# Query transposes of one batch moved from DMA to TensorE, and DMA engines put into the planned order, in a block-sorted attention with a bilinear feed-forward layer

## The chip, the cores and the metric

The kernel runs on one core of a Trainium2 chip. A core has five engines that each work through their own list of instructions in order: TensorE (PE, matmuls into PSUM banks), VectorE (DVE), ScalarE (ACT), GpSimd (POOL) and SyncE (SP). Here SP computes nothing and only issues DMAs; GpSimd issues DMAs too, besides tensor work. The DMAs of both are carried out by the core's 16 DMA engines. The metric is the device time of one execution in microseconds (us), lower is better.

## The reference

The inputs are q, k and v of shape (4 batches, 8 heads, 768 positions, 64), a matrix `sort_net` of 8 x 8 for each batch and head, and three weights of a feed-forward layer. Cut to what matters:

```python
P = sort_net
for _ in range(5):                      # rows, then columns, made to sum to one
    P = exp(P - P.max(-1)); P = P / P.sum(-1); P = P / P.sum(-2)
k_sorted = einsum('bhij,bhjcd->bhicd', P, k_b)      # blocks of 96 positions, mixed by P
v_sorted = einsum('bhij,bhjcd->bhicd', P, v_b)
attn = softmax(q_b @ k_sorted^T / 8)                # each block attends to its own block
x = (attn @ v_sorted) -> (4*768 tokens, 8*64)
out = ((x @ w_a) * (x @ w_b)) @ w_out               # 512 -> 1536 -> 512
```

## The kernel before

**Tiles and stages.** The work goes batch by batch (b = 0 to 3). In each, attention is done for four pairs of heads (p = 0 to 3), two heads of 64 filling the 128 partitions. For one pair, k and v are mixed by P on TensorE (`mix_pe` L480, `v_tok` L530), the query is transposed so that the head dimension lies on the partitions, scores and exponentials are made in two halves of four blocks (`scores_pe` L564, `exp_act` L578), the product with v follows (`o_pe` L585), and DVE normalizes it into a buffer `xp` (L594, L598). A transpose puts `xp` into `xT`, the input of the feed-forward layer.

**The feed-forward layer.** Batch 0 is done plainly (`ab_plain` L741). Batches 1 to 3 use a scheme of seven block products instead of eight (`ab_strassen` L806), with sums of the weights made once on GpSimd (`w_sums` L765) and sums of `xT` made for each batch (`x_sums` L785). The last product (`out_plain` L889) makes six output tiles per batch, and each is stored with two DMAs on SP (L915). While the outputs of batch b are made, attention of batch b+2 is done between them, and then the Strassen products of batch b+1 follow.

**How v and q travel.** For batches 1 to 3, v is mixed with positions on the partitions, copied out of PSUM by DVE, written to DRAM by a DMA on SP (`v_out` L540) and read back in another layout by a second one (`v_back` L544). The write-and-read is one round trip, both legs in SP's queue. `xp` of these batches is transposed by a DMA on SP (`x_dma` L615). The query has two ways. In batches 0 and 1 it is loaded plainly (L402), transposed on TensorE against an identity matrix (`q_pe` L463) and copied out of PSUM (`q_copy` L474). In batches 2 and 3 (`QDMA`, L194) it is loaded with the two heads interleaved (`q_wide` L350, two DMAs of small pieces for a pair of heads) and transposed by a DMA on SP (`q_dma` L620); `scores_pe` then reads it with another stride.

**What sets the order.** No engine's order is written by hand. Each piece of work is an `Op` with an engine or a choice of engines, an estimated duration, a latency until its result can be used, dependencies, buffers that it takes (`get`) and gives back (`put`), and a rank. `Plan.solve` (L132) simulates: it repeatedly takes the piece that can start first, and among those that can start within a small margin of one another (`EPS`, L40) the one of lowest rank. The resulting times are thrown away; the order stays, and `emit` (L988) writes every engine's instructions in that order. On the chip each engine follows its list and waits where a wait is due, however the real durations turn out. So a change of an estimate changes the order of real instructions on all engines.

GpSimd's loads are two pieces in the plan: an issue on POOL and a transfer on a made-up engine "DQ", `nbytes / 333e3` us long (`load`, L311), one transfer at a time. DMAs on SP, before the change, are one piece on SP with a fixed latency behind it; they do not occupy DQ. SP's stretch for a q transpose is 1.8 us with 3.6 us of latency (L662), for an x transpose 1.35 and 2.6 (L724), for the v write 0.5 and the default 2.3, for the v read 0.7 and 3.5 (L642, L643).

Of the kernel before, what the change touches and what calls it, by code (L numbers as in the profile page):

```python
# [35 lines left out]
class Plan:  # L36


    LAT = {"NIL": 0.0, "PE": 0.21, "ACT": 0.07, "DVE": 0.07, "POOL": 0.1, "SP": 2.3, "DQ": 1.9}
    EPS = {"NIL": 0.0, "PE": 0.08, "ACT": 0.04, "DVE": 0.04, "POOL": 0.04, "SP": 0.04, "DQ": 0.0}  # L40

    AT = {"NIL": 0.0, "PE": 0.8, "ACT": 2.05, "DVE": 0.8, "POOL": 1.25, "SP": 0.7, "DQ": 1.5}

# [5 lines left out]
    def add(self, eng, dur, fn, deps=(), get=(), put=(), rank=0.0, lat=None):  # L49
        alts = dict(eng) if isinstance(eng, (list, tuple)) else {eng: dur}  # L50
        op = Op(alts, fn, deps, list(get), list(put), rank, lat, len(self.ops))
        for key in op.put:
            self.holders[key] = self.holders.get(key, 0) + 1
        self.ops.append(op)
        return op
# [135 lines left out]

STRASSEN_AB = (1, 2, 3)
STRASSEN_OUT = ()
QDMA = lambda b, p: b >= 2  # L194
VDMA = lambda b, p: b >= 1


# [1 line left out]
def kernel(  # L199
# [40 lines left out]
    add = plan.add  # L240
# [70 lines left out]
    def load(fn, nbytes, deps=(), get=(), rank=0.0, many=0.0):  # L311
        ds = [d for d in deps if d is not None] + ([ld_n[-7]] if len(ld_n) >= 7 else [])
        i = add("POOL", 0.72 + many, fn, ds, get=get, rank=rank, lat=0.0)
        d = add("DQ", nbytes / 333e3, None, [i], rank=rank)
        ld_n.append(d)
        return d

    o_p = add("SP", 0.1, lambda: nc.sync.dma_start(
        out=p_nat, in_=sort_net.rearrange("b h i j -> (b h) i j")), lat=1.5)
    o_im = add("DVE", 0.1, lambda: nc.vector.memset(ident, 0.0))  # L320
# [17 lines left out]
    o_pads = add("DVE", 1.0, pads, rank=1)  # L338


    q_in, k_in, v_in = {}, {}, {}
# [8 lines left out]
    def q_wide(b, p):  # L350
        t = buf(("q2", b, p))
        for e in range(2):
            nc.gpsimd.dma_start(
                out=_ap(t, e * D, [[2 * W, P], [2 * D, NCH], [1, D]]),
                in_=_ap(q, (b * H + 2 * p + e) * S * D, [[W, P], [D, NCH], [1, D]]))
# [6 lines left out]
    NB_KV = 2 * S * D * 4  # L362
# [31 lines left out]
    def load_pair(b, p, rank, after=None):  # L394
        for name, t, into in (("k2", k, k_in), ("v2", v, v_in)):
            into[b, p] = load(lambda name=name, t=t: kv(b, p, name, t), NB_KV, [after],
                              get=[(name, (name, b, p))], rank=rank)
        if QDMA(b, p):
            q_in[b, p] = load(lambda: q_wide(b, p), NB_KV * 1.5, [after],
                              get=[("q2", ("q2", b, p))], rank=rank, many=0.9)  # L400
        else:
            q_in[b, p] = load(lambda: nc.gpsimd.dma_start(  # L402
                out=buf(("q2", b, p)),
                in_=_ap(q, (b * H + 2 * p) * S * D, [[W, P], [S * D, 2], [1, W]])), NB_KV,
                get=[("q2", ("q2", b, p))], rank=rank)
# [39 lines left out]
    for p in range(1, HP):  # L445
# [3 lines left out]
        put=["pc"], rank=-7)  # L449
# [175 lines left out]
    def mix_part(b, p, rk, split):  # L625

        pair = ("pair",)
        tc_o = VDMA(b, p)
        km = add("PE", 0.46, lambda: mix_pe(b, p, "k"), [k_in[b, p], s_ok[b, p]],
                 get=[("pair", ("km", b, p))], put=[("k2", b, p)], rank=rk)  # L630
        ks = []
        for h in ((0, 1) if split else (None,)):
            ks.append(add("ACT", 0.48 if split else 0.8,
                          lambda h=h: mix_copy("ACT", b, p, "k", h, tc_o), [km, o_pads] + ks,
                          get=[("kT", ("kT", b, p))] if not ks else [], put=[("km", b, p)],
                          rank=rk + (0.3 if h == 1 else 0)))
        if tc_o:
            vm = add("PE", 0.33, lambda: v_tok(b, p), [v_in[b, p], s_ok[b, p]],
                     get=[("pair", ("vm", b, p))], put=[("v2", b, p)], rank=rk)
            vc = add("DVE", 0.95, lambda: v_tok_copy("DVE", b, p), [vm],  # L640
                     get=[("vm", ("vb", b, p))], put=[("vm", b, p)], rank=rk)
            vo = add("SP", 0.5, lambda: v_out(b, p), [vc], put=[("vb", b, p)], rank=rk)  # L642
            vb = add("SP", 0.7, lambda: v_back(b, p), [vo, o_pads], get=[("vs", ("vs", b, p))],  # L643
                     rank=rk, lat=3.5)
            return ks, [vb]
        vm = add("PE", 0.46, lambda: mix_pe(b, p, "v"), [v_in[b, p], s_ok[b, p]],
                 get=[("pair", ("vm", b, p))], put=[("v2", b, p)], rank=rk + 0.05)
        vs = []
        for h in ((0, 1) if split else (None,)):
            alts = (("DVE", 0.56), ("ACT", 0.48)) if split else (("DVE", 0.95), ("ACT", 0.8))  # L650
            op = add(alts, None, None, [vm, o_pads] + vs,
                     get=[("vT", ("vT", b, p))] if not vs else [], put=[("vm", b, p)],
                     rank=rk + (0.3 if h == 1 else 0.05))
            op.fn = lambda h=h, op=op: mix_copy(op.eng, b, p, "v", h, tc_o)
            vs.append(op)
        return ks, vs
# [2 lines left out]

    def q_part(b, p, h, rk, after=None):  # L660
        if QDMA(b, p):
            st["q", b, p] = add("SP", 1.8, lambda: q_dma(b, p), [q_in[b, p]],  # L662
                                get=[("qT", ("qT", b, p))], put=[("q2", b, p)], rank=rk, lat=3.6)
            return st["q", b, p]
        qi = q_in[b, p, h] if (b, p, h) in q_in else q_in[b, p]
        pe = add("PE", 0.38 if h is not None else 0.5, lambda: q_pe(b, p, h), [qi, o_ident, after],
                 get=[("bank", ("qp", b, p, h))], put=[("q2", b, p)], rank=rk)
        alts = (("ACT", 0.48),) if h == 0 else (("ACT", 0.48), ("DVE", 0.36)) if h == 1 else (
            ("ACT", 0.8), ("DVE", 0.55))
        op = add(alts, None, None, [pe, first.get(("q", b, p))],  # L670
                 get=[("qT", ("qT", b, p))] if h in (0, None) else [],
                 put=[("qp", b, p, h)], rank=rk)
        first["q", b, p] = op
        op.fn = lambda: q_copy(op.eng, b, p, h)
        return op
# [41 lines left out]
    def attention(b, p, rk):  # L717
        qd = q_part(b, p, None, rk)
        ks, vs = mix_part(b, p, rk, False)
        if not VDMA(b, p):  # L720
            vs = [v_part(b, p, None, vs[0], rk)]
        ms = [so_part(b, p, h, False, ks[0], qd, vs[0], rk + 0.5 + 0.1 * h) for h in range(2)]
        st["last", b, p] = ms[1]
        d = add("SP", 1.35, lambda: x_dma(b, p), ms + [x_home(b)], put=[("xp", b, p)],  # L724
                rank=rk + 0.7, lat=2.6)
        for h in range(2):
            xT_done.setdefault((b, h), []).append(d)

# [160 lines left out]
    def out_plain(b, t, c, rk, last=False):  # L889
        key = ("po", b, t, c)  # L890

        def mm(ms):
            po = buf(key)
            for m in ms:
                nc.tensor.matmul(po, lhsT=hT[:, t * 2 + m // G, m % G, c * P:(c + 1) * P],  # L895
                                 rhs=w_out_sb[:, m, :], start=(m == 0), stop=(m == KO - 1),
                                 skip_group_check=True)
        early = [m for m in range(KO) if m % G < G - 1]
        late = [m for m in range(KO) if m % G == G - 1]
        early = [0] + early[1:]  # L900

        def h(ms):
            return [o for m in ms for o in h_done[b, t, m]]
        pe = add("PE", 0.215 * len(early), lambda: mm(early), h(early) + wo_in,
                 get=[("bank", key)], rank=rk)
        pe = add("PE", 0.215 * len(late), lambda: mm(late), h(late) + [pe], rank=rk - 0.5)
        out_last.setdefault(b, []).append(pe)
        op = add((("ACT", 0.59), ("DVE", 0.69)), None, None, [pe], get=[("o", ("o", b, t, c))],
                 put=[key], rank=rk)
        op.fn = lambda: copy(ENG[op.eng], buf(("o", b, t, c)), buf(key))  # L910

        def store():
            o_sb = buf(("o", b, t, c))
            for u in range(2):
                nc.sync.dma_start(  # L915
                    out=_ap(out, (b * S + t * NBH * BLK + 2 * c + u) * DMODEL,
                            [[NCH * DMODEL, NBH * CG], [1, DMODEL]]),
                    in_=o_sb[u * NBH * CG:(u + 1) * NBH * CG])
        add("SP", 1.2, store, [op], put=[("o", b, t, c)], rank=rk)


    plan.slots("chain", 4)
# [136 lines left out]
```

## Time and profile before

| | |
|---|---|
| median of 7 runs | 250.97 us (249.79 to 252.05) |
| the profiled execution, own time | 251.16 us |
| its span, first to last instruction | 249.4 us |
| mean granted TensorE clock | 0.985 of full |
| TensorE busy | 233.1 us, 93% of the span |
| DVE / ACT / POOL busy | 153.1 / 121.0 / 121.5 us |
| DMA, GpSimd's queue (q0) | 29,296 packets, 14.16 MB |
| DMA, SP's queue (q1) | 31,024 packets, 14.96 MB |
| DMA transposes of q / of x | 8, median 3.5 us to landing / 12, 2.9 us |

How to read it. A row of the page's list of groups gives line, engine, operation, output and inputs by the program's names, shapes and count; behind the first bar the busy time in us and the mean of one in ns, behind the second the idle time of the engine just before them and what ended it. A row of the timeline begins with its start and its length in us. "SPq" is SP issuing a DMA. In the digits of section 2, 40 slices of 6.2 us each show tenths of busy time. A view by windows gives for each stretch its length and then the busy time of PE, PEld (weight loads), DVE, ACT and POOL with counts, then the granted clock, the DMA share and GB/s. In the DMA view a share is the time of packets relative to that of 16 engines, and as packets overlap, it can pass 100%.

### The profile page before, as it was taken

To read this page: it belongs to the slowest core of one execution; us is meant where nothing else is said; L and a number is where in the kernel's file an instruction comes from. 1 tells how busy PE (TensorE), PEld (TensorE's weight loads), DVE (VectorE), ACT (ScalarE), POOL (GpSimd) and SP (SyncE) were. 2 spreads that over 40 slices of the span, in tenths; PEclk is the share of its full clock that TensorE was granted. 3 is DMA by queue.
4 is the path that set the end of the run, shared out by engine and by line. 5 is a ranking of instruction groups with operands and counts; after the bars stand their busy time and mean duration, and the time that the engine had idled before them with its cause. 6 is when DMAs were issued, how large, how long until landed. Compare 5 with 4: busy or idle time off the path is not lost.

```text
span 249.4 us, 5557 instructions
## 1 busy us (share of the span) xinstructions
PE 233.1 (93%) x2120; PEld 131.5 (53%) x2120; DVE 153.1 (61%) x351; ACT 121.0 (49%) x237; POOL 121.5 (49%) x133
## 2 busy tenths in 40 slices
PE   7898999994699999999999979899999999999992
PEld 2466766662366455565554535465654455565440
DVE  6656654652367456778998355688876149787120
ACT  3266647363066342576752542666641157664110
POOL 8879999995996003029954030066150004445000
PEclk9999999999599999999999999999999999999999
DMA  5999999999996997708999799300034550000135
GB/s 64 177 203 178 203 202 177 172 200 195 144 160 137 175 173 184 184 8 85 139 150 123 127 186 261 76 0 3 0 63 79 123 117 0 1 3 0 42 87 126
DMA packets 60346, 29.47 MB, mean 118 GB/s; under 512 B 39840, under 2 KB 57248, under 8 KB 60320
## 3 DMA queue, kind: packets, MB, share of 16 engines
q0 software_dynamic: 29296, 14.16, 45.4%
q1 hardware_dynamic: 31024, 14.96, 29.3%
q8 instruction: 17, 0.28, 0.5%
q14 instruction: 9, 0.07, 0.1%
HBM read 30.68 MB, written 8.65 MB: 158 GB/s over the span
## 4 chain that ended last, share of the span: by engine, by line
PE 84%; DMA 10%; POOL 2%; issue 1%; DVE 1%; ACT 0%; DVEq 0%
PE ps L827 33%; PE ps L895 23%; PE ps L745 13%; DMA vs<-vd 4%; PE ps L589 3%; PE ps L574 3%; DMA q<-in_q_dram 2%; PE ps L496 2%; PE ps L485 2%; PE ps L533 2%; DMA xT<-xp 2%; PE ps L979 1%; PE ps L469 1%; DMA vd<-vm 1%; PE ps L555 1%
## 5 line engine op out<-in xcount | busy, mean ns | idle before, releaser
L306 POOL TENSOR_TENSOR hT<-a,f 128x384 bf16<-128x384 bf16 x36 | 32.9, 918 | 73.4 <-DVE f L306 70.4
L895 PE MATMUL ps<-w_out_sb,hT 128*128 128x512 bf16 x288 | 66.0, 380 | 0.0
L836 ACT COPY f<-ps 128x384 f32<-128x384 f32 x108 | 48.1, 482 | 21.8 <-PE ps L827 19.1
L895 PEld LDWEIGHTS <-hT 128*128 128x128 bf16 x288 | 27.4, 98 | 30.9
L579 ACT ACTIVATE eT<-ps 96x768 bf16<-96x768 f32 x32 | 25.0, 806 | 21.0 <-PE ps L574 18.5
L306 DVE TENSOR_TENSOR f<-f,ps 128x384 f32<-128x384 f32 x54 | 29.1, 547 | 7.9 <-PE ps L827 5.7
L306 DVE TENSOR_TENSOR a<-f,ps 128x384 bf16<-128x384 f32 x54 | 29.5, 549 | 6.9 <-ACT f L836 3.3
L306 DVE TENSOR_TENSOR hT<-a,ps 128x384 bf16<-128x384 bf16 x42 | 23.1, 549 | 14.0 <-PE ps L745 6.6
L827 PE MATMUL ps<-tx,ws_b 128*128 128x384 bf16 x108 | 25.1, 327 | 0.0
L827 PE MATMUL ps<-tx,ws_a 128*128 128x384 bf16 x108 | 24.5, 327 | 0.0
L248 ACT COPY o<-ps 128x512 f32<-128x512 f32 x13 | 7.5, 586 | 33.4 <-PE ps L895 30.1
L250 DVE COPY o<-ps 128x512 f32<-128x512 f32 x11 | 7.6, 691 | 24.6 <-PE ps L895 24.5
L751 ACT CAST a<-ps 128x384 bf16<-128x384 f32 x24 | 11.5, 478 | 22.6 <-PE ps L745 19.5
L600 DVE TENSOR_TENSOR xp<-ps,rec 96x512 bf16<-96x512 f32 x32 | 21.7, 683 | 0.7
L745 PE MATMUL ps<-xT,w_a_sb 128*128 128x384 bf16 x96 | 20.2, 335 | 0.0
L745 PE MATMUL ps<-xT,w_b_sb 128*128 128x384 bf16 x96 | 20.2, 335 | 0.0
L589 PE MATMUL ps<-vs,eT 96*128 96x66 bf16 x256 | 12.8, 197 | 7.3 <-DMA vs<-vd 7.1
L827 PEld LDWEIGHTS <-ws_a 128*128 128x128 bf16 x144 | 13.6, 98 | 10.4 <-ACT f L836 1.4
L827 PEld LDWEIGHTS <-ws_b 128*128 128x128 bf16 x144 | 13.7, 97 | 9.6 <-ACT f L836 0.3
L306 POOL TENSOR_TENSOR tx<-xT,tx 128x768 bf16<-128x768 bf16 x2 | 4.4, 2194 | 27.4 <-DVE xp L600 18.3
L827 PE MATMUL ps<-xT,w_b_sb 128*128 128x384 bf16 x72 | 17.4, 327 | 0.0
L827 PE MATMUL ps<-xT,w_a_sb 128*128 128x384 bf16 x72 | 17.4, 326 | 0.0
(87 smaller groups left out, 340.6 us busy)
## 6 DMA issues: line engine op xcount, KB each, us to landing
out_dram<-o SPq DMA_DIRECT2D x48, 128.0 KB, 2.4
k<-in_k_dram POOLq DMA_DIRECT2D x16, 192.0 KB, 6.4
v<-in_v_dram POOLq DMA_DIRECT2D x16, 192.0 KB, 6.7
q<-in_q_dram POOLq DMA_DIRECT2D x24, 96.0 KB, 6.6
vd<-vm SPq DMA_DIRECT2D x12, 192.0 KB, 3.3
vs<-vd SPq DMA_DIRECT2D x12, 192.0 KB, 3.2
w_a_sb<-in_moe_w_a_dram POOLq DMA_DIRECT2D x4, 384.0 KB, 7.3
w_b_sb<-in_moe_w_b_dram POOLq DMA_DIRECT2D x4, 384.0 KB, 8.8
```

Source lines behind the costliest of these rows:

```text
L248: nc.scalar.copy(out=out, in_=in_)
L250: eng.tensor_copy(out=out, in_=in_)
L306: ENG[eng].tensor_tensor(out=out, in0=in0, in1=in1, op=op)
L574: nc.tensor.matmul(sc[:, e, i * BLK:(i + 1) * BLK], lhsT=kT[e * D:(e + 1) * D, at:at + P], rhs=rhs, start=True, stop=True)
L579: nc.scalar.activation(out=buf(("eT", b, p, h))[:, :, 0:HB], in_=buf(("sc", b, p, h))[0:BLK, :, 0:HB], func=AF.Exp, scale=float(scale))
L589: nc.tensor.matmul(ops_[:, e, i * OW:(i + 1) * OW], lhsT=eT[:, e, i * BLK:i * BLK + P], rhs=vs[:, h * NBH + i, e * OW:(e + 1) * OW], start ...
L600: nc.vector.tensor_tensor(out=_ap(xp, h * NBH * 2 * D, [[NB * 2 * D, BLK], [D, 2], [2 * D, NBH], [1, D]]), in0=_ap(ops_, 2, [[1024, BLK], ...
L745: nc.tensor.matmul(pf[:, 0:HW], lhsT=w_sb[:, kc, m * P:(m + 1) * P], rhs=buf(("xT", b))[:, kc, t * HW:(t + 1) * HW], start=(kc == 0), stop ...
L751: ea = add("ACT", 0.48, lambda: nc.scalar.copy(out=buf(("a", b, t, m)), in_=buf(("pf", b, t, m, "a"))[:, 0:HW]), [pa], get=[("a", ("a", b, ...
L827: nc.tensor.matmul(buf(key)[:, 0:HW], lhsT=lf(j), rhs=rf(j), start=start and j == 0, stop=j == 1, skip_group_check=not start)
L836: return add("ACT", 0.48, lambda: nc.scalar.copy(out=buf((name, b, g, n)), in_=buf(kA)[:, 0:HW]), [dep], get=[("f", (name, b, g, n))], rank=r)
L895: nc.tensor.matmul(po, lhsT=hT[:, t * 2 + m // G, m % G, c * P:(c + 1) * P], rhs=w_out_sb[:, m, :], start=(m == 0), stop=(m == KO - 1), sk ...
```

## The change

Four things change, and one follows from them.

1. `QDMA` is true for batch 3 alone. Batch 2's query is loaded plainly, one DMA for a pair instead of two, and transposed on TensorE with a copy out of PSUM, as in batch 1.
2. A helper `sp_dma` splits a DMA of SP into an issue on SP and a transfer on DQ, the engine that stands for the DMA engines in the plan. The v write and read, the q and x transposes and the output stores use it. In the plan all of these and GpSimd's loads now share DQ, one at a time. The transfers get rank -100, so they pass loads that could start within the margin.
3. The margin of DQ goes from 0 to 0.5 us.
4. The planned transfer of a wide q load is taken as 2.0 instead of 1.5 times that of a plain load.

What follows is a new order of the instructions on every engine from the second half of batch 0 on. The DMAs themselves, other than batch 2's q, are the same.

```diff
-    EPS = {"NIL": 0.0, "PE": 0.08, "ACT": 0.04, "DVE": 0.04, "POOL": 0.04, "SP": 0.04, "DQ": 0.0}
+    EPS = {"NIL": 0.0, "PE": 0.08, "ACT": 0.04, "DVE": 0.04, "POOL": 0.04, "SP": 0.04, "DQ": 0.5}
...
-QDMA = lambda b, p: b >= 2
+QDMA = lambda b, p: b >= 3
...
+    def sp_dma(issue, work, fn, deps, get=(), put=(), rank=0.0):
+        i = add("SP", issue, fn, deps, get=get, rank=rank, lat=0.6)
+        return add("DQ", work, None, [i], put=put, rank=rank - 100.0, lat=1.5)
...
-            q_in[b, p] = load(lambda: q_wide(b, p), NB_KV * 1.5, [after],
+            q_in[b, p] = load(lambda: q_wide(b, p), NB_KV * 2.0, [after],
...
-            vo = add("SP", 0.5, lambda: v_out(b, p), [vc], put=[("vb", b, p)], rank=rk)
-            vb = add("SP", 0.7, lambda: v_back(b, p), [vo, o_pads], get=[("vs", ("vs", b, p))],
-                     rank=rk, lat=3.5)
+            vo = sp_dma(0.35, 0.6, lambda: v_out(b, p), [vc], put=[("vb", b, p)], rank=rk)
+            vb = sp_dma(0.35, 0.9, lambda: v_back(b, p), [vo, o_pads],
+                        get=[("vs", ("vs", b, p))], rank=rk)
...
-            st["q", b, p] = add("SP", 1.8, lambda: q_dma(b, p), [q_in[b, p]],
-                                get=[("qT", ("qT", b, p))], put=[("q2", b, p)], rank=rk, lat=3.6)
+            st["q", b, p] = sp_dma(1.3, 1.6, lambda: q_dma(b, p), [q_in[b, p]],
+                                   get=[("qT", ("qT", b, p))], put=[("q2", b, p)], rank=rk)
...
-        d = add("SP", 1.35, lambda: x_dma(b, p), ms + [x_home(b)], put=[("xp", b, p)],
-                rank=rk + 0.7, lat=2.6)
+        d = sp_dma(1.3, 1.3, lambda: x_dma(b, p), ms + [x_home(b)], put=[("xp", b, p)],
+                   rank=rk + 0.7)
...
-        add("SP", 1.2, store, [op], put=[("o", b, t, c)], rank=rk)
+        sp_dma(1.2, 0.8, store, [op], put=[("o", b, t, c)], rank=rk)
```

## The prediction

> **What bounds the kernel now.** I read the page first, then the chain, then the waits, then the timeline around each wait of TensorE.
>
> ```profile
> PE 233.1 (93%) x2120; PEld 131.5 (53%) x2120; DVE 153.1 (61%) x351; ACT 121.0 (49%) x237; POOL 121.5 (49%) x133
> PE   7898999994699999999999979899999999999992
> PEclk9999999999599999999999999999999999999999
> PE 84%; DMA 10%; POOL 2%; issue 1%; DVE 1%; ACT 0%; DVEq 0%
> ```
>
> TensorE is the bound: 93% of the span, 84% of the chain. Time can be won only where it stands still, and every matmul added costs its full length. The digits that fall are the start, slice 11 (with the clock at half), slices 24 and 25 and the tail. The timeline names the waits (in brackets: idle before, and what ended it):
>
> ```profile
> 57.34 0.33 SPq L546 DMA_DIRECT2D vs<-vd  x1
> 64.54 1.04 PE L589 MATMUL ps<-vs,eT 96*128 96x66 bf16 x16 [5.83 <-DMA vs<-vd]
> ...
> 147.34 0.53 PE L485 MATMUL ps<-s_all,k 128*64 128x128 bf16 x12 [1.33 <-DVE vm L250]
> ...
> 159.88 0.67 PE L589 MATMUL ps<-vs,eT 96*128 96x66 bf16 x16 [1.05 <-DMA vs<-vd]
> ```
>
> All are DMA waits. Stall 1 (5.83 us) is the way of the first v of batch 1 through DRAM: written at 50.91, read at 57.34, there at 64.5. The 1.33 us is DVE standing in a tensor sum that waits for the last x transpose of batch 2, with the copy behind it that frees a PSUM pair. The 1.05 us is the last v of batch 3; another v wait of 0.26 us stands at 155.34. Stall 1 costs more than itself:
>
> ```profile
> 59.00:61.00 2.00, 0.00 (x0) 0.00 (x0) 0.00 (x0) 0.27 (x1) 0.59 (x1) 1.00 1.51 193
> 61.00:63.00 2.00, 0.00 (x0) 0.00 (x0) 0.00 (x0) 0.00 (x0) 1.98 (x3) 0.55 1.55 227
> ...
> 66.00:68.00 2.00, 2.00 (x7) 0.73 (x5) 1.25 (x4) 0.00 (x0) 2.00 (x3) 0.50 1.53 149
> 68.00:70.00 2.00, 2.00 (x32) 1.40 (x32) 0.72 (x2) 1.77 (x3) 2.00 (x3) 1.00 1.59 193
> ```
>
> (TensorE's busy time is third from the left, the granted clock third from the right.) The clock is halved from 61.2 to 68.0; the work of 64.5 to 68.0 takes twice as long, some 1.7 us lost. The DMA share, next to last, stands above 1 through the stall.
>
> **The sum's base.** The profiled execution took 251.16 us, its span 249.4 with 1.8 us around it; the median of the runs is 250.97. I sum differences in the span and add them to the median.
>
> **1. Query transposes of batch 2 on TensorE.** Nearest row is the same operation for batch 1:
>
> ```profile
> L469 PE MATMUL ps<-ident,q 128*64 128x128 bf16 x48 | 2.1, 223 | 0.0
> L250 DVE COPY qT<-ps 128x768 bf16<-128x768 bf16 x3 | 1.7, 558 | 1.1 <-PE ps L469 1.1
> L248 ACT COPY qT<-ps 128x768 bf16<-128x768 bf16 x1 | 0.8, 798 | 0.0
> ```
>
> 48 more such matmuls. On the chain twelve take 0.46 us, or 0.34 us where they overlap their neighbour: 4 pairs give 1.4 to 1.84, I take **+1.7**. The Trainium skill ("TensorE: Matmul & The Clock Gate", Part 4) speaks against this: about 275 ns per full transpose in a kernel, and a PSUM copy after it. 48 x 275 ns would be 13 us. The row's mean of 223 ns is near that, but it is one instruction's latency: twelve overlap to 0.46 us, so the chain's number decides.
>
> The copies are 0.80 us on ScalarE and 3 x 0.56 on DVE. ScalarE (5.39 of 10 us busy from 80 to 90) hides its one. In the new order, as the built program has it, the third and fourth pair are late: at the first Strassen products of batch 1 (102.85 us) two score halves, a v product with its normalizing, a v copy and the last query copy are still to come that lay ahead before. DVE, 7.39 of 10 us busy from 100 to 110, gets 0.56 + 0.96 + 0.88 more, so 9.8 of 10: its cover is all but gone and the Strassen sums behind it hold PSUM banks. Bounds 0 and 2.4 us, **+0.5** taken, since DVE is busy 9.29 of 10 at 120 to 130 with TensorE at 10.0.
>
> **2. Four DMA transposes leave SP's queue.** Four issues of 1.21 to 1.30 us, and their waits for q. Behind them stood v reads, stores and the last x transpose of batch 1, which I expect at 91 instead of 94.10. Nobody waits for that: TensorE has no idle time between 65 and 145 us, and its sums are done at 101.2 before 102.85. Worth 0.
>
> **3. The q loads of batch 2 get plain.** GpSimd issues one DMA of 0.73 us per pair for two of 0.83; the saved 3.7 us only let weight sums end earlier, 30 us ahead of use. 1,536 small packets a pair become 256 large ones. Does that shorten stall 1? This is the DMA view for 58 to 62 us:
>
> ```profile
> DMA packets 2707, 0.77 MB, mean 192 GB/s; under 512 B 2159, under 2 KB 2707, under 8 KB 2707
> q0 software_dynamic: 2196, 0.61, 146.9%
> q1 hardware_dynamic: 511, 0.16, 19.3%
> ```
>
> The engines are taken by GpSimd's queue, and small packets are most of it. But only one pair of q loads lies ahead of the v read (issued at 48.6); ahead of it stand three w_out loads as before, and the v write (50.91 to 57.27) goes through before any small packet moves. Replacing that pair by 256 large packets saves about 1 us of backlog (in these landings a plain load follows the one before it by 1.0 us, a wide pair by 2.0). The skill ("DMA: Bandwidth & Descriptors", Queues, rings and completion order) says that an engine takes turns between queues packet by packet. That speaks against a gain: each 256-byte packet of the v read (768 of them) would wait for a 768-byte packet instead of a 128-byte one, some 80 against 31 ns. The row has both queues moving together, as the rule says. By the rule alone, with backlog all through, 48 turns per engine longer by 49 ns are +2.4 us, less with several packets in flight; by the backlog -1. Bounds: +1.0, and the 4.4 us that the v write of 70.39 needed in lighter traffic, which is -2.8 and, with a stall too short for the clock to fall (2.5 us after the last matmul here), -4.5. I take **-0.5**.
>
> **4. Batch 3's stage, reordered.** The planner now gives DMA a shared, slower time, so the order gives TensorE other work first. The loads of batch 3 start on GpSimd behind products of the first Strassen groups: 113.4 before, within 0.5 of it after. SP still has all four query transposes in front of the x transposes, and the last of these waits for the same loads: landing stays at 145.8. But the PSUM pair is now wanted three matmul groups later, near 149, and the copy is done at 148: the **1.33 goes**.
> The first v product of batch 3 came at 150.77. Now: 150.77 - 1.33 + 0.5 (one more tail of an output tile before it) + 1.7 + 0.5 - 0.5 = 151.6. Its v read left at 147.59 and took 3.15. In the new order three stores stand in front instead of two, 1.2 us a pair of DMAs: 148.8 + 3.15 = 151.95. Stall 0.35.
> The last v read now stands behind the last store of batch 1. That output tile ends at 151.95 + 0.26 + 2.16 + 0.78 + 0.5 = 155.7; copy 0.8, store 1.2: read at 157.7, there 3.3 later (3.15 to 4.06 seen here), 161.0. TensorE gets there after 11 Strassen pieces of 0.325, three score halves and two v products, 155.7 + 4.9 = 160.6. Stall 0.4. So 2.64 us of stalls become 0.75: **-1.9**.
>
> **Sum.** +1.7 + 0.5 - 0.5 - 1.9 = -0.2 us, and the rest (Strassen of batches 2 and 3, outputs, tail) has the same work. 250.97 - 0.2 = **250.8 us**.
>
> **Rivals.** (a) *Stall 1 opens*, because packets, not bytes, filled the engines. For: 2,159 of 2,707 packets are small. Against: the write leg is unchanged, and one pair alone lies in front. The v read lands as that write did, in 4.4 us: 2.3 us more than forecast and part of the half clock: 248 us, 246.8 if the clock never falls. (b) *Slower: v reads stuck behind stores.* For: SP is in order, both reads of step 4 stand behind stores, and margins are under 0.5 us. If under that traffic each takes 5.9 us like the read of 65.72 instead of 3.2, TensorE waits 2.7 longer at the first or at the last: 253.5. It decides from the moment that a read lands after 151.6 or 160.6. Against: these reads met little GpSimd traffic before. (c) *The reorder moves no stall*: 2.64 us stay and the transposes are paid: 250.97 + 1.7 + 0.5 - 0.5 = 252.7. Against: the order visibly puts more work before the pair and the v products.
>
> **How the numbers follow.** Chances: the forecast 0.36, (a) 0.34, (b) and (c) together 0.30. A measurement of this kernel can tell about 0.5%, 1.25 us. Forecast alone: 249.7 to 252.2, which is "same". (a) is faster, (b) and (c) are slower. Cutting about a tenth at each side, 247.6 to 253.8.
>
> **What would show it.** Right: 96 matmuls on line 469's pattern instead of 48 and four DMA transposes of q; stall 1 at 4.8 to 6 us, clock half until about 68; no idle over 0.3 us between 65 and 100; no 1.3 us wait for a DVE copy near 147; waits for v reads of 0.3 to 1 us near 152 and 161. Wrong: stall 1 under 4 us (a); a v wait over 1.5 us in the last batch (b); the wait behind the tensor sum still there (c); TensorE idle at 103 to 112 over 1 us, which would make step 1's 0.5 too small.

## The result, and the profile after

The changed kernel took 252.37 us (median of 27 runs, 250.11 to 253.81), the kernel before 250.89 us beside it (64 runs). The ratio is 1.0069, with a 95% interval of 1.005 to 1.0087: slower by 1.3 to 2.2 us, where 250.8 us, 0.2 us faster, had been forecast. The time lies inside the range given (247.6 to 253.8), on the other side of no change. Intervals compare the fast executions of both kernels, as some took several us longer in a slower state (up to 258.18 us in one run below), so a ratio can differ a little from that of the medians. The profiled execution took 253.09 us with a span of 251.3 us, against 251.16 and 249.4 before, so this pair of profiles shows a little more than the medians do: 1.9 us.

The page of the kernel after:

```profile
PE 237.3 (94%) x2168; PEld 132.1 (53%) x2168; DVE 154.4 (61%) x355; ACT 122.9 (49%) x239; POOL 114.8 (46%) x127
PE   7998999993799999999999999999999999999992
PEclk9999999999589999999999999999999999999999
...
q0 software_dynamic: 24112, 14.16, 42.1%
q1 hardware_dynamic: 27824, 14.17, 26.9%
...
PE 91%; DMA 5%; POOL 1%; issue 1%; ACT 1%; DVE 0%
```

The parts of the change that the text had named are there: 48 more matmuls, 5,184 fewer packets on GpSimd's queue, and TensorE's row no longer dips in slices 24 and 26 (24 and 26, not 24 and 25, hold the waits at 147 and 159). The chain has gone from 84% to 91% TensorE. It waits less and still ends later.

The view of TensorE's waits of the kernel after (what waits, for what; us in total, times, the longest) has four rows:

```profile
PE ps L593 <- DMA vs<-vd: 5.9, 1, 5.9
PE ps L983 <- DVE warm_sb L326: 1.3, 1, 1.3
PE ps L500 <- issue: 1.1, 1, 1.1
PE ps L473 <- DMA q<-in_q_dram: 0.6, 1, 0.6
```

The first is stall 1, no shorter than before; the other three are the start of the kernel. The waits of batch 3 (1.33, 0.26 and 1.05 us) are gone without any of the remainders forecast. The timeline at stall 1, of the kernel after:

```profile
56.65 0.33 SPq L550 DMA_DIRECT2D vs<-vd  x1
...
64.34 1.04 PE L593 MATMUL ps<-vs,eT 96*128 96x66 bf16 x16 [5.91 <-DMA vs<-vd]
```

The v read left 0.7 us earlier than before and took 7.65 us instead of 7.16. A part of the DMA view for those 7.65 us, GpSimd's queue (packets, MB, share of 16 engines):

```profile
q0 software_dynamic: 1464, 1.05, 93.0%
```

The windows in and behind it (busy PE third number from the left, granted clock third from the right, DMA share next to last):

```profile
58.00:61.00 3.00, 0.43 (x3) 0.14 (x2) 0.44 (x1) 0.99 (x2) 3.00 (x3) 1.00 1.31 216
61.00:63.00 2.00, 0.00 (x0) 0.00 (x0) 0.00 (x0) 0.00 (x0) 1.98 (x3) 1.00 1.08 200
63.00:65.00 2.00, 0.66 (x13) 0.66 (x13) 0.03 (x1) 0.00 (x0) 1.99 (x3) 0.66 0.67 87
65.00:67.00 2.00, 2.00 (x13) 1.08 (x11) 1.22 (x4) 0.00 (x0) 2.00 (x3) 0.50 1.24 188
67.00:69.00 2.00, 2.00 (x25) 1.29 (x25) 0.91 (x2) 0.72 (x2) 1.99 (x2) 0.50 1.06 156
69.00:70.50 1.50, 1.50 (x12) 0.70 (x9) 0.35 (x1) 1.26 (x2) 1.48 (x3) 0.51 1.17 176
```

The half clock lies from 63.65 to 70.48, as long as before (6.83 us) but later: 6.1 us of TensorE's running time fall into it instead of 3.5, and about 3.1 us are lost instead of 1.7.

**A ledger of TensorE.** Where TensorE never idles, waits can't explain a loss. So I took its records one by one, from the third q transposes of batch 1 (near 68 us) to its end, and split the time from each start to the next. *Work* is each matmul at the usual step inside a group of its kind: output 216 ns, products and the v mix 163, k mix and q transpose 28.5 on average, scores 21.5, product with v 32.5. An *edge* is the step in which TensorE passes from one kind to another, where one of them is a small group (k mix and q transposes count as one kind, scores as another); what it takes beyond the usual step is its cost. *Stalls* are gaps over 0.12 us with the refilling behind them. What lies under the half clock is counted in its own column. (The last matmul's own 0.38 us completes each row.)

| kernel | total | work | edges: number, us | stalls: number, us | half clock | rest |
|---|---|---|---|---|---|---|
| before | 176.70 | 167.84 | 44, 4.48 | 3, 3.16 | 0.00 | 0.84 |
| after | 178.54 | 169.21 | 60, 6.41 | 0, 0.00 | 1.31 | 1.23 |

The difference of 1.84 us is 1.37 (48 transposes), 1.93 (16 more edges), -3.16 (stalls), 1.31 (half clock behind 68 us) and 0.39. The edges can be read in the timeline. Of the kernel before, batch 2's attention between outputs:

```profile
83.13 0.53 PE L485 MATMUL ps<-s_all,k 128*64 128x128 bf16 x12
83.59 0.50 PE L533 MATMUL ps<-v,s_all 128*128 128x384 bf16 x2
83.92 0.59 PE L895 MATMUL ps<-w_out_sb,hT 128*128 128x512 bf16 x2
```

And of the kernel after:

```profile
85.90 0.50 PE L537 MATMUL ps<-v,s_all 128*128 128x384 bf16 x2
86.33 0.34 PE L578 MATMUL ps<-qT,kT 64*128 64x96 bf16 x8
86.61 0.61 PE L899 MATMUL ps<-w_out_sb,hT 128*128 128x512 bf16 x2
87.15 0.34 PE L578 MATMUL ps<-qT,kT 64*128 64x96 bf16 x8
...
89.96 0.61 PE L899 MATMUL ps<-w_out_sb,hT 128*128 128x512 bf16 x2
90.40 0.67 PE L593 MATMUL ps<-vs,eT 96*128 96x66 bf16 x16
```

Subtract starts. Two v mixes (before) took 0.33 us ahead of outputs (83.59 to 83.92), and 0.43 ahead of scores (after, 85.90 to 86.33). In the kernel after, two outputs took 0.44 us ahead of a product with v (89.96 to 90.40), and 0.54 ahead of scores (86.61 to 87.15). The other side of a small group costs as much: inside a group of scores a pair of them takes 42 ns, and the last one before wide work 135. So in these records a small group alone between wide work takes some 0.2 us more than one beside its like. No page row shows it, since the mean of a group hides where it stands.

### The profile page after: what moved, and what is told of

Same layout as the page of the kernel before. It is cut to its first block, busy times and chain, and to the rows that moved or that the text cites. A ratio compares the mean times of both kernels' runs of the same rounds, so it can differ in the third digit from the quotient of the medians.

```text
span 251.3 us, 5639 instructions
## 1 busy us (share of the span) xinstructions
PE 237.3 (94%) x2168; PEld 132.1 (53%) x2168; DVE 154.4 (61%) x355; ACT 122.9 (49%) x239; POOL 114.8 (46%) x127
## 4 chain that ended last, share of the span: by engine, by line
PE 91%; DMA 5%; POOL 1%; issue 1%; ACT 1%; DVE 0%
PE ps L831 33%; PE ps L899 25%; PE ps L749 13%; PE ps L593 4%; PE ps L578 3%; DMA vs<-vd 3%; PE ps L983 2%; PE ps L473 2%; PE ps L537 2%; PE ps L489 2%; PE ps L500 2%; DMA q<-in_q_dram 2%; PE ps L559 1%; PE ps L612 1%; POOL k L362 0%
## 5 line engine op out<-in xcount | busy, mean ns | idle before, releaser
L306 POOL TENSOR_TENSOR hT<-a,f 128x384 bf16<-128x384 bf16 x34 | 31.0, 918 | 80.2 <-DVE f L306 80.0
L248 ACT COPY o<-ps 128x512 f32<-128x512 f32 x14 | 8.1, 585 | 34.7 <-PE ps L899 31.6
L250 DVE COPY o<-ps 128x512 f32<-128x512 f32 x10 | 6.9, 689 | 22.4 <-PE ps L899 22.4
L749 PE MATMUL ps<-xT,w_a_sb 128*128 128x384 bf16 x96 | 20.3, 335 | 0.0
L250 DVE CAST vm<-ps 128x768 bf16<-128x768 f32 x12 | 11.5, 956 | 12.3 <-PE ps L537 7.3
L248 ACT CAST kT<-ps 128x768 bf16<-128x768 f32 (+1 forms) x17 | 11.9, 705 | 13.3 <-PE ps L489 12.2
```

Of the source, the lines that this page charges most:

```text
L248: nc.scalar.copy(out=out, in_=in_)
L250: eng.tensor_copy(out=out, in_=in_)
L306: ENG[eng].tensor_tensor(out=out, in0=in0, in1=in1, op=op)
L749: nc.tensor.matmul(pf[:, 0:HW], lhsT=w_sb[:, kc, m * P:(m + 1) * P], rhs=buf(("xT", b))[:, kc, t * HW:(t + 1) * HW], start=(kc == 0), stop ...
```

## The experiments

They came in four series, each timed beside the kernel before on one chip; the medians of before in the four were 251.03, 251.04, 249.95 and 250.87 us. In some traces a few output records are missing; ledger rows are given only for complete ones.

**First series: the parts alone.** The transposes alone, in the kernel before (its planner then makes a new order for this too):

```diff
-QDMA = lambda b, p: b >= 2
+QDMA = lambda b, p: b >= 3
```

> One part alone: batch 2's query is loaded plainly and transposed on TensorE, with the old planning of DMAs. Theory A (the transposes cost more than the 1.7 us that were allowed, because their copies and score halves disturb TensorE's list): 3 us or more above the kernel before. Theory B (the transposes cost 1.7 to 2.2 us and the rest of the loss is the half clock after stall 1, which falls differently from run to run): 1.7 to 2.2 us above. Theory C (the loss is in the new order, not in the transposes): within 1 us of the kernel before.

Measured: 253.44 us, ratio 1.0079 (1.0052 to 1.0106), that is +2.0 us. Its profile is of an execution of 256.58 us and says little of the usual time, but it shows which waits there were (a row of its waits, and one of its timeline):

```profile
PE ps L589 <- DMA vs<-vd: 8.8, 2, 7.1
...
100.17 0.42 PE L589 MATMUL ps<-vs,eT 96*128 96x66 bf16 x8 [1.73 <-DMA vs<-vd]
```

The two waits for v are stall 1 and one in batch 2. The three of batch 3 are gone here too, without the new planning of DMA. The planner with DMA as a resource, with q as before:

```diff
-QDMA = lambda b, p: b >= 3
+QDMA = lambda b, p: b >= 2
```

> The other part alone: DMAs of SP share the DMA engines in the plan, margin 0.5, the wide load at 2.0, but batches 2 and 3 keep their query transposes on DMA. Theory A and B: the new order takes the stalls of batch 3 away and costs nothing else, 1 to 2.5 us below the kernel before. Theory C: 1 us or more above it, since the planner now believes in waits for DMA and spreads the work on TensorE.

Measured: 251.41 us, ratio 1.0004 (0.9975 to 1.0033). The kernel after once more:

> The changed kernel as it is, once more, for a second profile beside the others. Theory B: the clock is at half for another length of time after stall 1 (3.4 to 6.8 us of it with matmuls running), and the span moves by half of the difference. Theories A and C: nothing of note, the same ratio of 1.007 and a half clock of the same length.

Measured: 252.88 us, ratio 1.0062 (1.0032 to 1.0092), with stall 1 at 6.16 us and the half clock from 63.03 to 69.85. And the kernel after with half of the weight sums (tensor work on GpSimd) ahead of batch 2's loads in GpSimd's list, called "quiet" below:

```diff
-                    op = add(al, None, None, dj, rank=rank)
+                    op = add(al, None, None, dj, rank=rank if c else 22.0)
```

> The changed kernel with one rank altered: half of the weight sums go ahead of batch 2's loads on GpSimd, so these loads start some 7 us later; the lists of TensorE, DVE and ScalarE stay as they are. If batch 2's loads are what makes the first v round trip of batch 1 slow: stall 1 falls from 5.9 us to under 2.5, the clock stays whole, and the kernel is 5 to 8 us faster than the changed one. If the three loads of w_out ahead of them are enough to make it slow: stall 1 stays over 4 us and the time within 1 us.

Measured: 251.81 us, ratio 1.0038 (1.0007 to 1.0069). Its profile has stall 1 at 2.76 us and a half clock of 3.41 us only behind it. The edit did less than expected: the first load of batch 2 left at 49.61 us instead of 46.64, not 7 us later, and by 56.4 us as many had left as in after.

The two parts add up within the noise: +2.0 and 0.0, where after is +1.5 to +1.7. The order, forecast to gain 1.9 us, gained nothing alone: the interval ends at -0.6 us. Added to the transposes it gained about 0.3 us by the two ratios, with an uncertainty of 0.8. The last run looked as if the loads' traffic made stall 1, but its profile was of its shortest execution (249.95 us); that needed another test.

**Second series: the price of an edge, of a transpose, and the loads again.** In the first of four, pieces of any kind in TensorE's finished list are moved next to their like (`c` is such a piece, `y` the place behind the last piece of its kind, up to five ahead):

```diff
-        return sorted(self.ops, key=lambda o: (o.start, o.seq))
+        return self.join(sorted(self.ops, key=lambda o: (o.start, o.seq)))
...
+                    if c.ready > order[y].start + SLACK or any(
+                            o in c.deps or hold(o) & hold(c) for o in order[y:pe[i]]):
+                        continue
+                    new = seq[:2] + [c] + seq[2:back + 1] + seq[back + 2:]
+                    if changes(new) >= changes(seq):
+                        continue
+                    order.insert(y, order.pop(pe[i]))
```

> The kernel after; in TensorE's finished list from the planner's time 60 on, a piece of work is put right behind an earlier piece of its own kind up to five places ahead, where its inputs are there and no buffer or bank forbids it: 21 fewer changes of kind out of 237, the same matmuls, the same transposes, the other engines' lists as far as they hang on it. Theory S (changing between kinds of work costs TensorE about 0.1 us each, read from the ledger: a token-order v mix takes 0.33 us right behind a k mix and 0.41 where it stands alone): 21 x 0.1 = 2.1 us less than after, 250.3 us, and TensorE's time from the first q transposes of batch 1 to its end 176.4 us where after has 178.5. Rival H (the order costs nothing by itself; what after lost beside its transposes is the phase of the half clock behind stall 1): the same as after, 252.4 +- 0.4, ledger 178.5. Rival L (a piece moved ahead waits for its inputs): slower than after by the stalls, gaps of 0.3 us and more in TensorE's work past 70 us.

Measured: 260.36 us, ratio 1.0359 (1.0336 to 1.0382): a miss, rival L. The edges fell from 60 to 50 and their cost from 6.41 to 5.28 us, but TensorE stood still eleven times, 7.1 us in the ledger:

```profile
PE ps L566 <- DVE vm L279: 1.1, 1, 1.1
PE ps L622 <- ACT eT L612: 0.6, 1, 0.6
PE ps L928 <- DVE hT L335: 0.6, 1, 0.6
PE ps L860 <- ACT f L869: 0.5, 2, 0.2
PE ps L607 <- ACT kT L277: 0.5, 1, 0.5
```

(five of its waits; 566 is the v mix, 622 the product with v, 928 the outputs, 860 Strassen, 607 scores). Next, every piece of q transposes of batch 2 is done twice:

```diff
-        pe = add("PE", 0.38 if h is not None else 0.5, lambda: q_pe(b, p, h), [qi, o_ident, after],
+        def twice():
+            for _ in range(2 if b == 2 else 1):
+                q_pe(b, p, h)
+        pe = add("PE", 0.38 if h is not None else 0.5, twice, [qi, o_ident, after],
```

> The kernel after with every piece of q transposes of batch 2 done twice over, into the same bank: the second result is the first one's, nothing is left out. It adds 4 x 12 transposes of 64 x 128 and no change of kind. If the transposes lie fully on the path at the row's price (0.46 us per twelve): +1.84 us against after, 254.2 us. If their price in the change came from breaking into other work (what is left of the 0.50 us per pair that the ledger shows is a change of kind), still 4 x 0.46, since the second dozen repeats the first: then the difference of 2.0 to 1.84 is the changes. If TensorE has slack in batch 2's and batch 1's stage that swallows them: under +0.5, 252.9 at most.

Measured: 253.82 us, ratio 1.0106 (1.0077 to 1.0136): about 1.0 us above after, and in the ledger 1.37 us more work with the same 60 edges. In the ledger a second dozen costs 0.34 us, not 0.46: the rest of the 0.46 was the edge. The ledger shows no slack that swallows them; in time the 1.0 us is barely clear of the noise. The quiet version of the kernel before, with the same line as above:

> The kernel before with half of the weight sums' loads and adds put ahead of batch 2's loads in GpSimd's list (rank 22 for the first half), and nothing else. Theory Q (stall 1 is the re-laid v of batch 1, whose 128-byte packets share the DMA engines with batch 2's loads; what is sent later shortens it): TensorE's gap near 58 us falls from 6.2 us to about 3, the half clock behind it is shorter, and the time falls by what the same edit took from after, 1.07 us (252.88 to 251.81): 249.9 us, ratio 0.996. If all of the gap came through to the end: 251.0 - 3 = 248. Rival (the short gap in the one profile of the quiet version of after was a lucky run): 251.0, ratio 1.000, gap 6 us.

Measured: 250.70 us, ratio 0.9976 (0.9953 to 1.0), stall 1 at 5.59 us. (The packets of the v read are of 256 bytes, not 128 as the expectation has it.) And the new planner with old q, quiet:

> The new planner with q of batches 2 and 3 still by DMA, and the weight sums as in the run before this: if the two add up, plan alone (251.41) less 1.1: 250.3, ratio 0.997. If the new order is worth nothing whatever stall 1 does, it equals the kernel before with the same edit within 0.4 us. If the new order was held back only by stall 1's half clock, it is 1.5 us or more under that run: 248.4.

Measured: 251.10 us, ratio 1.0009 (0.998 to 1.0039). Stall 1 stands at 5.92 us: sending half of the weight sums ahead doesn't open it, and 2.76 us had been chance. That does not refute theory Q, since the edit hardly thinned the traffic at the read. What the chance was can be seen in part: the two profiles with a short stall so far, 2.76 us and 3.99 us (doubled transposes), are the only two of after's variants with another 3.41 us at half clock from 26 us on. There the first v write left at 51.9 and 52.0 us instead of 50.63, and its read took 4.67 and 6.39 us. The last run's waits show where the order's gain went:

```profile
PE ps L593 <- DMA vs<-vd: 5.9, 1, 5.9
...
PE ps L831 <- DVE tx L306: 0.5, 1, 0.5
...
PE ps L831 <- ACT f L840: 0.3, 1, 0.3
PE ps L831 <- DVE vm L250: 0.2, 1, 0.2
```

The waits of batch 3 for v and for the copy are gone here too, and three new ones stand before Strassen products. (The plan alone without the quiet edit has the first two as well.)

**Third series: small groups alone are moved.** In the kernel after and in the kernel before, groups of q transposes, k mix and scores go forward to their like, only where their inputs had been there for 0.2 us; the code is that of the joined run with

```diff
+        small = lambda o: bool({"q_pe", "mix_pe", "scores_pe"} & set(o.fn.__code__.co_freevars))
...
+                if not small(c) or c.start < JOIN or small(order[pe[i - 1]]):
+                    continue
```

In the opposite direction ("parted"), wide work that is ready goes between two small neighbours:

```diff
...
+            if (c.start > PART and small(b) and small(c) and wide(d) and d.ready <= c.start - SLACK
+                    and not any(o in d.deps or hold(o) & hold(d) for o in order[y:z])):
+                order.insert(y, order.pop(z))
...
```

> The kernel after; in TensorE's finished list from the planner's time 60 on, a group of q transposes, k mix or scores is moved up to five places forward, right behind an earlier such group, where its inputs were there at least 0.2 us before and no buffer or bank forbids it; nothing else moves ahead. Theory S (an edge between such a small group and wide work costs TensorE 0.095 us: the last 163 ns step of wide work before a score group is 258 ns, the last 40 ns step of a score group before wide work 135 ns): edges in the list 58 to 47, so 11 x 0.095 = 1.05 us less than after: 251.3, ratio to before 1.002; TensorE's time from batch 1's third q transposes to its end, without stalls and without the half clock, 177.2 to 176.2. Rival H (the edges cost nothing, the steps are only where the profile puts the ends): 252.4, ratio 1.006 and 177.2. Rival L (as in the joined run, a piece moved ahead waits): stalls of 0.3 us and more behind 70 us, and slower than after.

> The kernel before; where two small groups (q transposes, k mix, scores) stand side by side in TensorE's finished list and the next piece of wide work was ready, that piece is put between them: 42 edges become 55, all instructions the same. Theory S: 13 x 0.095 = +1.24 us: 252.2, ratio 1.005; without stalls and half clock TensorE's time from batch 1's third q transposes on goes from 174.1 to 175.3. Rival H: 251.0, ratio 1.000, 174.1. Rival L (scores that come 0.3 us later make others wait): over 1.010, with the three stalls of batch 3 (2.6 us) longer.

> The kernel before with the same regrouping as in the first run of these four: 42 edges become 36. Theory S: -0.57 us: 250.5, ratio 0.998, 174.1 to 173.5 without stalls. Rival H: 251.0, ratio 1.000. Rival L: slower than before, by stalls.

> The run before this one with half of the weight sums put ahead of batch 2's loads on GpSimd, which alone gave 0.9976. If both hold and add up: -0.57 - 0.6 = 249.8, ratio 0.995, which would beat the kernel before and the kernel after. If the quiet version was chance: as the run before this one.

| kernel | us | ratio | total | work | edges | stalls | half clock | rest |
|---|---|---|---|---|---|---|---|---|
| after, recut | 253.70 | 1.0151 (1.0107 to 1.0195) | 178.54 | 169.21 | 49, 5.17 | 3, 2.00 | 0.18 | 1.61 |
| before, parted | 252.41 | 1.0113 (1.0085 to 1.0141) | 177.89 | 167.84 | 57, 5.83 | 3, 2.84 | 0.49 | 0.51 |
| before, recut | 252.72 | 1.0102 (1.0053 to 1.015) | 178.46 | 167.84 | 38, 3.92 | 7, 5.81 | 0.12 | 0.39 |
| before, recut, quiet | 252.75 | 1.0091 (1.006 to 1.0122) | 176.72 | 167.84 | 38, 3.76 | 5, 3.20 | 1.12 | 0.43 |
| plan alone, quiet | 251.10 | 1.0009 (0.998 to 1.0039) | 177.30 | 167.84 | 53, 5.65 | 3, 1.53 | 0.35 | 1.55 |

In the ledger the price holds in every list, 38 edges or 60: 0.106 to 0.112 us each. As time, only the parted run tests it, because its stalls did not grow in sum (2.84 us against 3.16). It is slower, as theory S said and against rival H, but by more than the 1.24 us expected: 2.8 us against the before of its series, which was about 1 us faster than in the others, where the ledger has +1.35 for edges and +1.19 in all. Its ratio also passes the 1.010 of rival L, of which the ledger shows no longer stalls in sum. So the sign is shown in time, the size is not. In the recut runs the saved edges were lost to waits that had not been there, rival L again; the recut after has the ledger total of after, 178.54, so its higher ratio isn't placed. The quiet edit brought nothing there either: 0.9976 had been chance, or does not add up. The waits of the recut kernel before, of which the second line is new:

```profile
PE ps L614 <- DMA vs<-vd: 7.2, 3, 5.6
PE ps L599 <- ACT eT L604: 1.8, 3, 0.8
```

The releaser is the exponential on ScalarE, which gives back the PSUM pair of earlier scores: scores moved ahead stand before it.

**Fourth series: stall 1 taken away.** What stayed open was stall 1. Here v of the first one or two pairs of batch 1 goes by batch 0's way, with no trip through DRAM; the planner orders anew.

```diff
-VDMA = lambda b, p: b >= 1
+VDMA = lambda b, p: (b, p) >= (1, 2)
```

(and `(1, 1)` for the first pair alone.)

> The kernel before, with v of the first pair of batch 1 by the way of batch 0 (mixed and transposed on TensorE, copies in PSUM's place of the way through DRAM); the planner orders anew around it. Theory R (stall 1 is the length of the round trip through DRAM, some 13.6 us from write to landing, of which TensorE has about 8 us of other work): the first trip is now that of the second pair, TensorE has about 1.3 us more work by then, stall 1 about 4 us with the half clock behind it: 251.0 - 2 + 1.0 for the dearer v = 250.0. Rival T (the traffic of batch 2's loads holds whatever round trip stands there): the gap stays near 6 us, and the time is 251.0 + 1.0 = 252.0.

> The kernel before, with v of the first two pairs of batch 1 on TensorE. Theory R: four score-and-product groups more are there to be worked on while the third pair's v travels: stall 1 under 2 us, no half clock behind 60 us, 251.0 - 4 to 6 - 1.7 + 2 x 1.0 = 245.5 to 247.5. Rival T: the stall stands before the third pair's product at 5 us or more, 252 to 253.

> The kernel after, with v of the first pair of batch 1 on TensorE. If stall 1 and the half clock behind it are what set after behind before (the phase of the half clock, 3.1 us lost against 1.7): it comes to within 0.5 us of the same edit of before. If the loss is in the later list (48 transposes, 1.4 us, and the edges of small groups): 1.5 us behind it, ratio 1.006 higher.

> The kernel after, with v of the first two pairs of batch 1 on TensorE. As in the run before this one: within 0.5 us of before with the same edit (stall 1 was the loss), or 1.5 us behind it (the later list is). With stall 1 gone and the transposes in place, 247 to 249.

| | us | ratio |
|---|---|---|
| before, one pair | 248.14 | 0.9846 (0.9798 to 0.9894) |
| before, two pairs | 245.93 | 0.9786 (0.9752 to 0.982) |
| after, one pair | 250.12 | 0.9947 (0.992 to 0.9973) |
| after, two pairs | 245.26 | 0.9756 (0.9727 to 0.9785) |

Both versions with two pairs beat both kernels; the last is the fastest of all, 7.1 us under the kernel after by the medians. Two times lie below every forecast: 248.14 (250.0 or 252.0) and 245.26 (247 to 249). Of the last version, the timeline and windows at the place of stall 1, and GpSimd's queue while the v read travelled (69.42 to 72.14):

```profile
69.42 0.33 SPq L550 DMA_DIRECT2D vs<-vd  x1
...
72.18 0.41 PE L593 MATMUL ps<-vs,eT 96*128 96x66 bf16 x8 [0.74 <-DMA vs<-vd]
```

```profile
68.00:70.00 2.00, 2.00 (x30) 1.24 (x24) 1.58 (x3) 1.09 (x2) 2.00 (x2) 1.00 0.71 107
70.00:72.00 2.00, 1.44 (x22) 0.77 (x21) 0.85 (x2) 1.67 (x3) 1.63 (x2) 1.00 0.69 192
```

```profile
q0 software_dynamic: 27, 0.02, 4.4%
```

The stall is 0.74 us and the clock stays whole. With one pair moved, the profile of the kernel before (an execution of 250.29 us, 2.2 above its median) still has it:

```profile
62.93 0.33 SPq L546 DMA_DIRECT2D vs<-vd  x1
...
70.46 1.04 PE L589 MATMUL ps<-vs,eT 96*128 96x66 bf16 x16 [4.94 <-DMA vs<-vd]
```

So each theory had a half of it. A read of the same size takes 7.48 us at 62.93, amid batch 2's loads (share of GpSimd's queue 112%), 5.21 us at 62.85 in the kernel after with one pair moved (75%), and 2.72 us at 69.42, when the loads have run out (4.4%, where it was 93% in the stall of after): the traffic stretches the trip, by near 5 us at most, as T says. But a trip that starts late enough gets out of it, and then theory R's numbers come true (245.5 to 247.5 expected of before with two pairs). Moving single loads by the little that the change and the quiet versions did wasn't enough.

And with two pairs after no longer trails: by the medians it lies 0.7 us ahead of before with the same edit, though the intervals overlap; with one pair, 2 us behind it. A fixed price of 1.5 us for the later list is refuted. This doesn't say which part of it went with stall 1, as the lists were planned anew.

## Why the prediction was wrong

**Step 1 (+1.7 and +0.5): near in the sum, in part by luck.** Alone it measured +2.0 us. The parts were different: 48 transposes are 1.37 us of work, and after has 7 more edges than the list of the plan alone (0.75 us). The +0.5 for DVE's cover didn't come: TensorE was never idle at 103 to 112. And the +2.0 us is that of a new list in which, by its one profile, batch 3's waits are gone as well; if its usual executions lack them too, the rest of that list cost some 4.6 us, and where is not shown. Of the transposes' own price, the choice of the chain's overlap was right: the 275 ns each of the Trainium skill ("TensorE: Matmul & The Clock Gate", Part 4) would have made 13 us, and twelve in a row take 0.34 us.

**Step 2 (0):** nothing in the runs speaks against it; it wasn't tried alone. The last x transpose of batch 1 left at 92.80, not at 91, and TensorE waited for none.

**Step 3 (-0.5): failed.** Stall 1 was 5.91 and 6.16 us in the two profiles of after, none shorter than before's 5.83 (2.76 and 3.99 in two variants, so it varies by itself). The small packets became fewer, but the v read still travelled amid loads. I had asked how long the queue ahead of it was; the fourth series shows that what counts is how much of the loads is running beside it. The rule of turns between queues (the Trainium skill, "DMA: Bandwidth & Descriptors", Queues, rings and completion order), which spoke against a gain, points the right way in that the gain didn't come: the read took 7.65 and 7.68 us in after, 7.16 before, 2.72 out of the traffic. But its +2.4 us didn't come either, and no run separates turns between queues from engines that are simply shared. My assumption that the half clock ends near 68 fell too, at 70.48: the profiled pair lost 1.3 us more to it.

**Step 4 (-1.9): failed, and it is the larger miss.** The waits went as forecast, and wholly: 3.16 us with the refilling. What the sum put at nothing is the price of the new order itself. I had priced each group by a row and treated the order as free. The plan alone (in the ledger of its quiet version) has 9 more edges than before (1.17 us), new small waits (1.53 us, three stalls) and 0.7 us of shorter ones, 3.4 us in all; measured, it is worth 0.0 us (-0.6 to +0.8) instead of -1.9. In the list of after itself the new stalls don't appear, and the ledger puts step 4 at -3.16, +1.0 for 9 edges and +0.4, near what was forecast; there the half clock makes up the 1.3 us. But not all of the 3.16 is the order's merit. The first v read landed at 153.07 where 151.95 was forecast, which would have been a stall of 1.5 us for a TensorE that came at 151.6; it came at 153.92, 2.3 us later than forecast. How much of the wait went by this lateness isn't shown, since the read hangs on earlier work too. And the transposes alone, in their profile, lost the waits without this step.

**The rivals.** Rival (c) gave 252.7, near the 252.37 measured, but by luck, as its mechanism was another: it kept the stalls, while the reorder removed all three of batch 3 and gave the time back elsewhere. (b) didn't happen: the late v reads landed at 153.07 and 162.58, later than the moments named, but TensorE came to them at 153.92 and 163.16 and waited for neither. (a) didn't happen in after; but taking stall 1 away is worth what it promised, and more.

**What stays open.** The half clock lost between 1.7 and 3.1 us in profiles of several lists, before-like and after-like, so I count most of the profiled pair's 1.3 us as chance. Then the ledger explains about 0.5 us of the medians' 1.5, and about one microsecond, in executions that were not profiled, isn't placed. Nor is it shown which of step 4's price and step 1's a given edge belongs to: the list of the transposes alone has 44 edges, as many as before.

## What to carry to other kernels

When an engine is at 94% and never idle, a ledger of start-to-start steps shows what no list of waits does: here a group of scores took about twice as long where wide work surrounded it, so count a new order's edges before crediting it with the stalls that it removes. A wait can also vanish only because the waiting engine has become later, and then nothing is gained. Moving pieces to save edges bought waits in all four tries. The stall in front of the round trip through DRAM opened when the trip was taken off the path and out of the traffic, not when a few loads were moved a little.

## What the runs showed of the hardware that was not expected

- **Edges.** A step from one kind of work to another, one of them a small group, took 0.106 to 0.112 us more than usual on average, in ten profiles of seven orders (0.095 from wide work into scores, 0.113 from scores into wide work in the kernel before); passing from wide work into a product with v, or from it into wide work, took 0.00 to 0.02 us more. Why is not shown.
- **The half clock.** Every recorded stretch at half clock behind stall 1 lasted 3.41 or 6.83 us, and began at a different time in each run (61.2, 61.6, 62.5, 63.7 and 64.0 us, where the stalls had begun between 58.2 and 59.8). Stalls of 2.76 and 3.99 us had 3.41 us of it, one of 2.95 and all of 4.9 us and more had 6.83; a stall of 0.74 us had none. In every trace each stretch at half clock begins a whole number of 3.41 us after the trace's first clock record, which itself lies anywhere from 4.0 to 7.3 us: 16 of these units in before (6.57 to 61.19), 17 in after (5.63 to 63.65). In before the unit from 57.77 to 61.19 held 0.94 us of TensorE's work, and the half clock followed it; in after the one from 56.83 to 60.24 held 1.60 us, the clock stayed whole, and the half clock followed the next, empty one. A stall of about the same length thus loses 1.7 to 3.1 us behind it by where the units fall; that is a part of the 3.7 us over which the runs of after spread.
